# The last step of a fused Mamba-2 and expert-mixture kernel: products in another order, the last block turned by TensorE and stored as whole rows

## Chip, cores and metric

One core of one Trainium2 chip. Time is device microseconds of the whole execution, the median of several. Ratios are the mean time of one kernel's fast runs over that of the other's of the same rounds, so they are not quite the ratio of the medians quoted. The rounds of the experiments ran on two chips, each round with its own runs of the kernel before.

## The reference

Two parts after each other. The first is a state-space scan over 4 x 8 heads, whose output becomes a matrix `x` of 3072 tokens by 256. The second is four experts, which take nearly all of the time:

```python
for e in range(E):                       # E = 4, F = 1024, D = 256
    h = np.maximum(x @ w1[e], 0.0)
    out += p[:, e:e + 1] * (h @ w2[e])   # out: [3072 tokens, 256]
```

Everything is float32.

## The kernel before

Tokens go through in six blocks of 512. A block takes eight steps, and each step (but the first two of all, which use plain products) makes seven first and seven second products of half-size matrices (a Strassen-like scheme: seven products and sums in place of eight products). The second products add up in PSUM over the eight steps, and lie there transposed: 128 features on the partitions, tokens along the row. After the last step of a block the sums are combined into `o` and stored. Only the very last block has nothing behind it to hide its end; `finish` is that end.

```python
def diff(n, o, x, y):                    # VectorE, line 385: operands of products 7, 5, 6, 4
    ...
    nc.vector.tensor_sub(h[o], h[x], h[y])

ORDER = (1, 3, 7, 5, 6, 2, 4)            # where product i adds up: acc[k, index // 2], half index % 2

def smul(n, i):                          # second product i: two matmuls, four instructions (L440)
    u, half = divmod(ORDER.index(i), 2)
    ...
    rhs = hid[n][("11", "21", "22", "T4", "T1", "T2", "T3")[i - 1]]   # T3, T1, T2, T4 come from diff
    for j in range(JJ):
        nc.tensor.matmul(out=acc[k, u][:, half], lhsT=w2_op(n, w)[:, j], rhs=rhs[:, j], ...)

def finish(n):
    ...                                  # b1, b2: first and second 256 tokens
    for i in (6, 1, 3):
        smul(n, i)
    keep(k, 0)                           # ScalarE copies acc[k, 0] to SBUF
    p1, p3 = kept[k, 0][:, 0], kept[k, 0][:, 1]
    add(u[:, 0], acc[k, 2][:, 0], p1)
    add(u[:, 1], u[:, 0], p3)
    smul(n, 7)
    smul(n, 5)
    p7, p5 = acc[k, 1][:, 0], acc[k, 1][:, 1]
    add(u[:, 2], p7, u[:, 0])            # L489
    add(o[:, 1, b2], p5, u[:, 2])        # L490
    add(o[:, 0, b2], p5, u[:, 1])
    leave(k, HB, HB, (nc.sync, nc.scalar))
    smul(n, 2)
    add(o[:, 0, b1], acc[k, 2][:, 1], p1)
    smul(n, 4)
    add(o[:, 1, b1], acc[k, 3][:, 0], u[:, 2])   # L496
    leave(k, 0, HB, (nc.sync, nc.scalar))

def leave(k, lo, n, queues):
    ot = ffn.tile([P, 2, n // 32, 32], FP32, tag="ot", name="ot")
    nc.vector.transpose(ot.rearrange("p d b j -> p d (b j)"), o[:, :, lo:lo + n])   # 32x32 blocks
    dst = out[r:r + n].rearrange("(b i) (d a j) -> a d i b j", i=32, j=32, d=2)
    for q in range(P // 32):
        for d in range(2):
            queues[d].dma_start(out=dst[q, d], in_=ot[32 * q:32 * q + 32, d])       # runs of 128 B
```

`ot` holds the transposed values in blocks of 32 by 32, as its rearrangement shows, so a run of memory that can be written at once is 32 floats, 128 bytes.

Of the kernel before, what the change touches and what calls it, by code (L numbers as in the profile page):

```python
# [8 lines left out]
FP32 = mybir.dt.float32  # L9
# [3 lines left out]
P = 128  # L13
# [4 lines left out]
def kernel(  # L18
# [33 lines left out]
    nc = tc.nc  # L52

    NCH, _, W = xbc.shape
    E, DM, F = w1.shape
    NH = NQ * NT
    HN = P
    BLK = 512
    HB = BLK // 2
# [16 lines left out]
    att = ctx.enter_context(tc.tile_pool(name="att", bufs=2))  # L76
    ffn = ctx.enter_context(tc.tile_pool(name="ffn", bufs=2))
    ps_att = ctx.enter_context(tc.tile_pool(name="ps_att", bufs=2, space=bass.MemoryType.PSUM))
# [59 lines left out]
    def w2_op(n, w):  # L138

        if w < 4:  # L140
            a_, d = divmod(w, 2)
            return wt2[n][:, :4 * HB].rearrange(
                "p (a j d m) -> p a j d m", a=2, j=JJ, d=2)[:, a_, :, d]
        return wt2[n][:, w * HB:w * HB + HB].rearrange("p (j m) -> p j m", j=JJ)
# [13 lines left out]
    def sum_w2(n):  # L158
# [7 lines left out]
        out=a_sb, in_=a.rearrange("c h s -> (c h) s").rearrange("(p r) s -> p r s", r=2))  # L166
# [7 lines left out]
    ident = const.tile([P, NH, P], FP32, name="ident")  # L174
# [13 lines left out]
    for q in range(NQ):  # L188
        r = slice(32 * q, 32 * q + 32)
# [199 lines left out]
    def begin(k, u):  # L389
        if (k, u) in acc:  # L390
            return False
        acc[k, u] = ps_s.tile([P, 2, HB], FP32, tag=f"acc{u}", name=f"acc{u}")
        return True
# [19 lines left out]
    def plain_second(n, b, d):  # L413


        k = n // SPB
        u, half = {(1, 1): (2, 1), (2, 1): (3, 0), (1, 2): (0, 1), (2, 2): (3, 1)}[d, b]
        begins = begin(k, u)
        for i, w in enumerate(((A11, A12), (S3, A22))[d - 1]):
            for j in range(JJ):  # L420
                nc.tensor.matmul(  # L421
                    out=acc[k, u][:, half], lhsT=w2_op(n, w)[:, j], rhs=hid[n][f"{i + 1}{b}"][:, j],
                    start=(begins and i == 0 and j == 0), stop=False, skip_group_check=True)

    def smul(n, i):

        if n < 0:
            return
        k = n // SPB
        if n < PLAIN:  # L430
            if n == PLAIN - 1 and i in ORDER[:4]:
                m, d = divmod(ORDER.index(i), 2)
                plain_second(m, 2, d + 1)
            return
        u, half = divmod(ORDER.index(i), 2)
        begins = begin(k, u)
        w = (A11, A12, S4, A22, S1, S2, S3)[i - 1]
        rhs = hid[n][("11", "21", "22", "T4", "T1", "T2", "T3")[i - 1]]
        for j in range(JJ):
            nc.tensor.matmul(  # L440
                out=acc[k, u][:, half], lhsT=w2_op(n, w)[:, j], rhs=rhs[:, j],
                start=(begins and j == 0),
                stop=(n % SPB == SPB - 1 and j == JJ - 1), skip_group_check=True)

    kept = {}

    def keep(k, u):
        e = kept[k, u] = ffn.tile([P, 2, HB], FP32, tag=f"kept{u}", name=f"kept{u}", bufs=1)
        nc.scalar.copy(out=e, in_=acc[k, u])
# [22 lines left out]

    def finish(n):

        k = n // SPB
        add = nc.vector.tensor_add
        b1, b2 = slice(0, HB), slice(HB, BLK)
        o = kept[k, "o"] = ffn.tile([P, 2, BLK], FP32, tag="o", name="o", bufs=1)
        u = ffn.tile([P, 3, HB], FP32, tag="u", name="u", bufs=1)
        for i in (6, 1, 3):  # L480
            smul(n, i)
        keep(k, 0)
        p1, p3 = kept[k, 0][:, 0], kept[k, 0][:, 1]
        add(u[:, 0], acc[k, 2][:, 0], p1)
        add(u[:, 1], u[:, 0], p3)
        smul(n, 7)
        smul(n, 5)
        p7, p5 = acc[k, 1][:, 0], acc[k, 1][:, 1]
        add(u[:, 2], p7, u[:, 0])  # L489
        add(o[:, 1, b2], p5, u[:, 2])  # L490
        add(o[:, 0, b2], p5, u[:, 1])
        leave(k, HB, HB, (nc.sync, nc.scalar))
        smul(n, 2)
        add(o[:, 0, b1], acc[k, 2][:, 1], p1)
        smul(n, 4)
        add(o[:, 1, b1], acc[k, 3][:, 0], u[:, 2])  # L496
        leave(k, 0, HB, (nc.sync, nc.scalar))

    def leave(k, lo, n, queues):

        o = kept[k, "o"]

        ot = ffn.tile([P, 2, n // 32, 32], FP32, tag="ot", name="ot")
        nc.vector.transpose(ot.rearrange("p d b j -> p d (b j)"), o[:, :, lo:lo + n])
        r = k * BLK + lo
# [3 lines that stand above are left out]
                queues[d].dma_start(out=dst[q, d], in_=ot[32 * q:32 * q + 32, d])  # L509
# [85 lines left out]
    for n in range(PLAIN, NS):  # L595
        k, r = divmod(n, SPB)
# [67 lines left out]
        if ending:  # L664
            combine(k - 1, 2)
    finish(NS - 1)


# [43 lines left out]
```

## Time and profile before

| | before |
|---|---|
| time, median of the 3 runs before the prediction | 664.66 us (664.35 to 665.47) |
| TensorE busy | 646.3 us of 662.1, 98% |
| end of the last matmul to the end of the span | 6.7 us |
| of that, store: first issue to end | 6.4 us |

The time is TensorE's, except for a ramp at the start and this tail. The lines are in the prediction. To compare tails of different executions I use one mark in all of them, which no edit touches: the start of VectorE's last pair of differences. In the kernel before, the timeline (start, duration, engine, line, operation) has it at

```profile
648.32 1.42 DVE L385 TENSOR_TENSOR hT<-h,hT 128x512 f32<-128x512 f32 x2
```

From there to the end of the span at 662.1 is the **tail**, 13.78 us. Spans are printed to 0.1 us, so a tail may be off by 0.05; with the unrounded spans of the packed traces none below moves by more than 0.04.

### The profile page before, as it was taken

What the parts mean: (1) busy time and instruction counts of PE and PEld (TensorE: products, weight loads), DVE (VectorE), ACT (ScalarE), POOL (GpSimd) and SP (SyncE); (2) the same over time, 40 slices, a digit from 0 to 9 for tenths busy, and PEclk for the clock granted to TensorE, in tenths of its full rate; (3) what the DMA queues carried; (4) which work ended last, traced back from release to release, by engine and by line L of the source; (5) the groups of instructions that cost most, each with busy time, mean ns of one, the idle gap of its engine ahead of it and who ended that gap; (6) DMA issues with size and microseconds to landing.
All of it is one profiled execution on the core that took longest, in us unless ns stands there. A gap on an engine that the chain in (4) does not pass through costs nothing.

```text
span 662.1 us, 8709 instructions
## 1 busy us (share of the span) xinstructions
PE 646.3 (98%) x3333; PEld 537.5 (81%) x3333; DVE 491.9 (74%) x788; ACT 114.2 (17%) x244; POOL 110.7 (17%) x153
## 2 busy tenths in 40 slices
PE   7999999999999999999999999999999999999995
PEld 2687887888888888888888888888888888888884
DVE  6857898788687688776878776868868767856554
ACT  2001111221112122111121111112211211111110
POOL 2587795030000002000003000002100000200000
PEclk9999999999999999999999999999999999999999
DMA  8985998636736444755372765454673543563102
GB/s 251 342 331 218 335 345 317 218 156 192 258 128 260 158 153 128 299 193 183 148 258 68 254 224 181 184 183 167 182 264 125 194 166 112 153 244 112 55 1 32
DMA packets 70937, 128.62 MB, mean 194 GB/s; under 512 B 29040, under 2 KB 52464, under 8 KB 70896
## 3 DMA queue, kind: packets, MB, share of 16 engines
q1 hardware_dynamic: 65968, 112.79, 49.9%
q0 software_dynamic: 2304, 14.68, 5.6%
q10 hardware_dynamic: 2624, 0.61, 0.4%
q8 instruction: 26, 0.43, 0.3%
q14 instruction: 15, 0.12, 0.1%
HBM read 109.99 MB, written 18.07 MB: 193 GB/s over the span
## 4 chain that ended last, share of the span: by engine, by line
PE 86%; DVE 8%; issue 1%; DMA 1%; DVEq 0%; SPq 0%
PE acc L440 38%; PE X L356 22%; PE Y L356 18%; DVE hT L385 3%; PE acc L421 2%; PE g L273 2%; PE y L301 1%; DVE MT L283 1%; DVE LT L239 1%; PE y L295 1%; DMA wt<-w_d 1%; PE X L404 1%; PE Y L404 1%; DVE z L368 1%; DVE h L378 1%
## 5 line engine op out<-in xcount | busy, mean ns | idle before, releaser
L440 PE MATMUL acc<-hT,wt 128*128 128x256 f32 x736 | 183.4, 382 | 0.8 <-DVE hT L385 0.8
L368 DVE TENSOR_TENSOR z<-Y,snap 128x512 f32<-128x512 f32 x138 | 95.0, 688 | 112.7 <-ACT snap L363 87.3
L363 ACT COPY snap<-X 128x512 f32<-128x512 f32 x138 | 80.8, 586 | 469.1 <-PE X L356 467.1
L440 PEld LDWEIGHTS acc<-hT,wt 128*128 128x128 f32 x736 | 138.2, 190 | 25.5 <-issue 6.3
L356 PE MATMUL X<-yS,wt 128*128 128x256 f32 x552 | 141.7, 379 | 0.0
L440 PE MATMUL acc<-h,wt 128*128 128x256 f32 x552 | 141.5, 379 | 0.0
L440 PEld LDWEIGHTS acc<-h,wt 128*128 128x128 f32 x552 | 104.9, 190 | 14.3
L356 PEld LDWEIGHTS X<-yS,wt 128*128 128x128 f32 x552 | 104.9, 190 | 14.3
L378 DVE SCALAR_TENSOR_TENSOR h<-z,gate 128x512 f32<-128x512 f32 x138 | 97.3, 705 | 3.1
L356 PE MATMUL Y<-yT,wt 128*128 128x256 f32 x368 | 94.7, 380 | 0.7 <-DVE z L368 0.6
L356 PEld LDWEIGHTS Y<-yT,wt 128*128 128x128 f32 x368 | 68.6, 190 | 12.3 <-DVE z L368 1.5
L385 DVE TENSOR_TENSOR hT<-h,hT 128x512 f32<-128x512 f32 x92 | 70.7, 768 | 3.2
L385 DVE TENSOR_TENSOR hT<-h,h 128x512 f32<-128x512 f32 x92 | 62.7, 718 | 0.7
L246 POOL TENSOR_TENSOR MT<-xb,LT 128x128 f32<-128x128 f32 x20 | 8.3, 414 | 318.0 <-issue 142.4
L239 DVE TENSOR_TENSOR_SCAN LT<-ab,ident 128x1024 f32<-128x1024 f32 x24 | 55.9, 2329 | 0.4
L356 PE MATMUL Y<-yS,wt 128*128 128x256 f32 x184 | 49.4, 391 | 2.1 <-DVE z L368 2.0
L283 DVE TENSOR_TENSOR MT<-g,LT 128x256 f32<-128x256 f32 x96 | 34.0, 416 | 21.0 <-PE g L273 20.8
L356 PE MATMUL X<-yT,wt 128*128 128x256 f32 x184 | 47.3, 380 | 0.5 <-DVE MT L283 0.5
L356 PEld LDWEIGHTS Y<-yS,wt 128*128 128x128 f32 x184 | 33.2, 189 | 11.0 <-DVE z L368 4.2
L378 DVE SCALAR_TENSOR_TENSOR h<-X,gate 128x512 f32<-128x512 f32 x50 | 34.5, 691 | 9.6 <-PE X L356 5.7
L356 PEld LDWEIGHTS X<-yT,wt 128*128 128x128 f32 x184 | 34.9, 190 | 5.6 <-DVE MT L283 0.9
L257 POOL TENSOR_TENSOR cts<-ctm,dec 128x256 f32<-128x256 f32 x20 | 14.6, 732 | 70.9 <-DVE dec L254 70.5
(77 smaller groups left out, 330.4 us busy)
## 6 DMA issues: line engine op xcount, KB each, us to landing
wt<-w_d SPq DMA_DIRECT2D x80, 896.0 KB, 6.2
w_d<-wt POOLq DMA_DIRECT2D x16, 896.0 KB, 6.2
ab<-acut_d SPq DMA_DIRECT2D x22, 512.0 KB, 9.8
wt<-in_w_dram SPq DMA_DIRECT2D x32, 256.0 KB, 5.6
xb<-in_xbc_dram SPq DMA_DIRECT2D x24, 320.0 KB
gate<-p_d SPq DMA_DIRECT2D x24, 256.0 KB, 6.0
out_dram<-ot SPq DMA_DIRECT2D x40, 64.0 KB, 2.0
ah<-ac_d SPq DMA_DIRECT2D x19, 64.0 KB
```

The lines of the kernel that those rows point to most:

```text
L239: nc.vector.tensor_tensor_scan(out=LT, data0=s["ab"], data1=ident.rearrange("p h s -> p (h s)"), initial=0.0, op0=ALU.mult, op1=ALU.add)
L257: nc.gpsimd.tensor_mul(cts, s["ctm"], dec.unsqueeze(1).to_broadcast([HN, NT, P]))
L273: nc.tensor.matmul(out=g.rearrange("p t s -> p (t s)"), lhsT=s["xb"][k, OBT:OBT + P], rhs=s["ctm"][k].rearrange("p t s -> p (t s)"), start ...
L283: nc.vector.tensor_mul(s["MT"][:, h, 0:P], s["g"][q], s["LT"][:, h])
L356: nc.tensor.matmul(out=f[bank][:, j], lhsT=wt1[n][:, w, j * P:j * P + P], rhs=rhs, start=(i in (1, 2, 5) and j == 0), stop=(j == JJ - 1), ...
L363: nc.scalar.copy(out=s, in_=first[n]["X"])
L368: nc.vector.tensor_add(z, first[n]["Y"], first[n][i])
L378: nc.vector.scalar_tensor_tensor(out=h, in0=first[n][src], scalar=0.0, in1=g.unsqueeze(1).to_broadcast([P, JJ, HB]), op0=ALU.max, op1=ALU. ...
L385: nc.vector.tensor_sub(h[o], h[x], h[y])
L404: nc.tensor.matmul(out=f[bank][:, j], lhsT=wt1[n][:, w, j * P:j * P + P], rhs=yT[k][:, i, cols], start=(i == 0 and j == 0), stop=(i == 1), ...
L421: nc.tensor.matmul(out=acc[k, u][:, half], lhsT=w2_op(n, w)[:, j], rhs=hid[n][f"{i + 1}{b}"][:, j], start=(begins and i == 0 and j == 0), ...
L440: nc.tensor.matmul(out=acc[k, u][:, half], lhsT=w2_op(n, w)[:, j], rhs=rhs[:, j], start=(begins and j == 0), stop=(n % SPB == SPB - 1 and ...
```

## The change

The intent: start the last seven products without the wait for a difference; drop the stream transposes and the sixteen stores of short runs; let TensorE turn `o` in full 128 by 128 blocks, so that a token's 256 features stand as one row of 1 KB, and store in three transfers.

```diff
-        for i in (6, 1, 3):
-            smul(n, i)
+        smul(n, 1)
+        smul(n, 3)
         keep(k, 0)
         p1, p3 = kept[k, 0][:, 0], kept[k, 0][:, 1]
+        smul(n, 6)
 ...
+        def turn_out(b, d):
+            if b not in turned:
+                turned[b] = ps_att.tile([P, 2, DM], FP32, tag="att", name="turned")
+                rows[b] = ffn.tile([P, 2, DM], FP32, tag="rows", name="rows")
+            for i in range(2):
+                lo = b * HB + i * P
+                nc.tensor.transpose(
+                    turned[b][:, i, d * P:d * P + P], o[:, d, lo:lo + P], ident[:, 0])
 ...
-        leave(k, HB, HB, (nc.sync, nc.scalar))
         smul(n, 2)
         add(o[:, 0, b1], acc[k, 2][:, 1], p1)
+        turn_out(1, 1)
         smul(n, 4)
+        turn_out(1, 0)
+        nc.scalar.copy(out=rows[1], in_=turned[1])
+        nc.sync.dma_start(out=dst(1), in_=rows[1])
+        turn_out(0, 0)
         add(o[:, 1, b1], acc[k, 3][:, 0], u[:, 2])
-        leave(k, 0, HB, (nc.sync, nc.scalar))
+        turn_out(0, 1)
+        nc.vector.tensor_copy(rows[0][:, 0], turned[0][:, 0])
+        nc.sync.dma_start(out=dst(0)[:, 0], in_=rows[0][:, 0])
+        nc.scalar.copy(out=rows[0][:, 1], in_=turned[0][:, 1])
+        nc.scalar.dma_start(out=dst(0)[:, 1], in_=rows[0][:, 1])
```

`dst(b)` is the 256 rows of that half, as `(i p) m -> p i m`. "First half" below is b = 0, "second half" is b = 1; the second is ready first.

More of the change, by code (lines that the diff above doesn't have):

```diff
@@ L477, in finish, with dst @@
         b1, b2 = slice(0, HB), slice(HB, BLK)
-        o = kept[k, "o"] = ffn.tile([P, 2, BLK], FP32, tag="o", name="o", bufs=1)
+        o = ffn.tile([P, 2, BLK], FP32, tag="o", name="o", bufs=1)
         u = ffn.tile([P, 3, HB], FP32, tag="u", name="u", bufs=1)
-        for i in (6, 1, 3):
-            smul(n, i)
+        turned, rows = {}, {}
+        def turn_out(b, d):
[6 more added lines that the diff above has]
+                    turned[b][:, i, d * P:d * P + P], o[:, d, lo:lo + P], ident[:, 0])
+        def dst(b):
+            r = k * BLK + b * HB
+            return out[r:r + HB].rearrange("(i p) m -> p i m", p=P)
+        smul(n, 1)
+        smul(n, 3)
         keep(k, 0)
         p1, p3 = kept[k, 0][:, 0], kept[k, 0][:, 1]
+        smul(n, 6)
         add(u[:, 0], acc[k, 2][:, 0], p1)
```

## The prediction

> **What bounds the kernel now.** I read the engine shares first, then the last 22 us of the timeline, because the change touches only the last of the steps. The page says that TensorE is the bound of the whole:
>
> ```profile
> PE 646.3 (98%) x3333; PEld 537.5 (81%) x3333; DVE 491.9 (74%) x788; ACT 114.2 (17%) x244; POOL 110.7 (17%) x153
> PE 86%; DVE 8%; issue 1%; DMA 1%; DVEq 0%; SPq 0%
> ```
>
> The first line is busy time of 662.1 us, the second the chain that ended last. Nothing in the change shortens the 98%; it can only shorten the tail after the matmuls. The comparison of instruction order shows the same: up to the last step each engine has the same instructions, in the same order, with the same waits. The timeline of the end, columns start, duration, engine, line, operation:
>
> ```profile
> 649.06 1.13 PE L440 MATMUL acc<-hT,wt 128*128 128x256 f32 x4 [0.85 <-DVE hT L385]
> ...
> 652.01 0.59 ACT L449 COPY kept<-acc 128x512 f32<-128x512 f32 x1 [9.22 <-PE acc L440]
> 652.63 0.42 DVE L484 TENSOR_TENSOR u<-acc,kept 128x256 f32<-128x256 f32 x1 [2.90 <-ACT kept L449]
> ...
> 653.68 0.42 DVE L489 TENSOR_TENSOR u<-acc,u 128x256 f32<-128x256 f32 x1 [0.17 <-PE acc L440]
> 654.14 0.42 DVE L490 TENSOR_TENSOR o<-acc,u 128x256 f32<-128x256 f32 x1
> 654.35 1.03 PE L440 MATMUL acc<-hT,wt 128*128 128x256 f32 x4
> ...
> 655.67 3.85 SPq L509 DMA_DIRECT2D out_dram<-ot  x8
> 655.67 3.94 ACTq L509 DMA_DIRECT2D out_dram<-ot  x8
> 655.88 0.41 DVE L496 TENSOR_TENSOR o<-acc,u 128x256 f32<-128x256 f32 x1
> 656.32 0.71 DVE L504 STREAM_TRANSPOSE ot<-o 128x512 f32<-128x512 f32 x1
> ```
>
> TensorE starts the last seven products at 649.06 after a wait of 0.85, because product 6, put first, needs a difference that VectorE ends at 649.02. It ends at 655.38. VectorE is done at 657.03. The last 5 us are the store: eight issues on each of two queues, until 659.6. The stretches and the DMA view from 640 on show what the transfers do:
>
> ```profile
> 657.10:659.70 2.60, 0.00 (x0) 0.00 (x0) 0.00 (x0) 0.00 (x0) 0.00 (x0) 1.00 0.85 132
> 659.70:662.10 2.40, 0.00 (x0) 0.00 (x0) 0.00 (x0) 0.00 (x0) 0.00 (x0) 0.72 0.30 47
> DMA packets 4352, 0.53 MB, mean 23 GB/s; under 512 B 4352, under 2 KB 4352, under 8 KB 4352
> ```
>
> The last two columns of the stretches are the DMA share and GB/s: engines 85% busy at only 132 GB/s, with every packet small (0.53 MB over 4352 is about 122 B). Data begins at 656.5, 0.83 after the first issue, and ends at about 660.7; at 131 GB/s 0.53 MB needs 4.0 us, which is that. So the end is bound by 128-byte stores, not by issuing. The wait of the sync queue agrees:
>
> ```profile
> SPq L708 <- DMA out_dram<-ot: 1.2, 1, 1.2
> ```
>
> It waited 1.2 us after its last issue, to 660.8; semaphores and a barrier of all engines fill the 1.3 us to 662.1, and stay.
>
> **What the Trainium skill says.** "DMA: Bandwidth & Descriptors", Specifications, names 512 B as the smallest transfer that reaches line rate. The trace agrees in kind: 131 GB/s here, with 128 B, while from 8.5 to 10.5 us packets mostly of 512 B and more ran at 334 GB/s. "TensorE: Matmul & The Clock Gate", Part 4, says that a TensorE transpose does 128x128 at once, lands in PSUM and needs a copy after, about 275 ns in a kernel for bf16. The one transpose in this trace, 96 columns of f32, has 314 ns and a weight load of 124, so 128 columns would load in about 165 (an estimate, 124 x 128/96). "PSUM — Partial Sum Buffer", PSUM bank collisions, says that two engines may not touch one bank in the same partitions at once, and that the compiler orders them. In the changed program ScalarE's copy of the second half waits for VectorE's copy of the first, as that would ask: both halves lie in one bank. No run yet shows its cost.
>
> **The change, part by part.**
>
> Order of products. 1 and 3 need only what is ready, so TensorE starts at 648.21 instead of 649.06, and 6 comes third at 649.94, past 649.02. A product takes 0.86 (four instructions of 0.215), its result is there 1.03 after it starts, and consumers began 0.13 (VectorE) to 0.19 (ScalarE) later. So product 5 starts at 651.66, product 2 at 652.53 and ends at 653.39. Gain 0.85 for all that follows.
>
> VectorE before the first transpose. The add of L489 waited for product 5, not 7 (653.55 + 0.13 = 653.68). In the new order: 651.66 + 1.03 + 0.13 = 652.82, then the o add of the second half ends 0.88 later (654.56 − 653.68) at 653.70, the next at 654.04, and the first half's first at about 654.45. No stream transpose lies between them any more: 0.71 twice is gone, and with it what delayed L496 by about 0.5.
>
> Transposes on TensorE. Eight of them, in four pairs. The first pair stands ahead of product 4 and waits until 653.75, so TensorE stands 0.35; then two weight loads of about 0.18 and that of product 4 before its first multiply, at 654.29. That gives back 0.05 of a 0.85 gain: product 4 began at 654.24 before. Its result: 654.29 + 1.03 = 655.32. The pairs for (second half, 0) and (first half, 0) run behind it, to about 655.85, beside the last add, which takes 655.45 to 655.86. The last pair starts at 655.90: two loads, then a multiply of 0.31, and 0.1 until seen, 0.36 + 0.31 + 0.1, so 656.65.
>
> Copies. ScalarE's copy of the second half (128x512; 0.586 for the same shape at L363) starts at about 655.8, ends at 656.4. VectorE's of 128x256 out of PSUM: 0.40, as its adds, to 657.05. ScalarE's then, 0.37 as at L308: to 657.45.
>
> Stores. 512 KB in three transfers instead of sixteen, 1 KB runs. Issues at 656.42 and 657.07 (sync), 657.5 (scalar); data 0.83 later: 657.25, 657.90 and 658.33. At some 300 GB/s (the mean of 4 to 12 us in this trace was 307) 256 KB take 0.87 and 128 KB 0.44, so the three end at 658.12, 658.56 and 659.0. The last transfer is no longer bound by the bandwidth but by its own late issue. Landing seen 0.1 after, 659.1, plus the unchanged 1.3: 660.4 to 660.5 in place of 662.1.
>
> Sum, by what ends the tail: the last block was turned at 657.03, and is now at 656.65, −0.4 (the order's gain is spent on the first pair's stall, so this comes from the two stream transposes). The two copies in a row that TensorE's transpose needs, +0.8. From the last write to SBUF to the landing 1.65 instead of 3.8, −2.1. Total about −1.7 us, 0.26% of the time. Predicted 664.66 − 1.7 = 663.0.
>
> **Rivals.**
>
> First, the tail becomes a chain of small steps. Add, transposes, two copies and an issue each hand over by semaphore; each handover that costs 0.1 to 0.2 more, or transposes that take 0.3 each instead of 0.18 at the margin, would eat 0.5 to 1.0. For it: nearly half of my sum is handovers, and the first pair stalls TensorE just where the old kernel ran. Against it: 0.02 to 0.17 is what the chain shows. It would make 663.5 to 664.0, no visible change.
>
> Second, the transfers are not faster. Stores of 1 KB into memory by themselves are nowhere in this trace; the 307 GB/s are mostly loads with much in flight. If the landing is a fixed latency near the 1.9 to 2.0 us seen from issue to landing for 32 and 64 KB pieces, the last lands at 657.5 + 2.0 = 659.5: 663.4. This is the one I fear most. At 131 GB/s still, 512 KB from 657.25 would end at 661.2, slower by 0.5: 665.1. The small packets with busy engines speak against that.
>
> Third, it goes better: data of 256 KB runs at 400 GB/s (slices of 422 and 436 stand around 158 us), transposes pack at half a matmul's time, the semaphores at the end shrink with sixteen transfers fewer. Then the landing is at 658.4, and the time 662.2.
>
> **Range and chances.** The middle is 663.0. The rivals put it between 662.2 and 664.0; the three runs before spread over 1.1 us by themselves, which I add in part: 661.8 to 664.4. A gain of over 2% would be 13 us, all of the span from the first of the seven products to the end. A loss of 2% would need a new wait of 13 us in an unchanged program, or a slow run. Faster 0.005, same 0.99, slower 0.005.
>
> **What would show it.** In the profile after: the products of the last step start with no wait on VectorE; product 4's matmuls start within 0.3 us of where they did; no packets of under 512 B after 650 us; the stretch with DMA is under 2 us long instead of 4.2; ScalarE's second copy starts just as VectorE's ends; from the last landing to the end is again 1.3. It is wrong if TensorE stands over 0.5 us at the first pair, if a pair takes over 0.7, if the last issue to landing is over 2 us, or if the time is above 664.4 with nothing changed before 648 us.

## The result, and the profile after

The median went from 664.5 us (4 runs) to 662.0 (4 runs, 661.11 to 663.06); ratio 0.9962, 95% interval 0.9939 to 0.9986. That is 2.5 us less, within 2%, and it is not a chance difference. Six more runs of the same kernel, on another occasion, gave 0.9977 (0.9962 to 0.9992). The tail went from 13.78 to 11.40 us, so 2.4 less. The other 0.4 between the two profiled spans (662.1 and 659.3) lies ahead of the mark, in unchanged instructions, and is not the change's. The first store is issued as late as before, 7.36 after the mark against 7.35: what the new order of products saves, the transposes and copies take up, and all of the 2.4 is won behind that issue.

The timeline after, from the mark on:

```profile
647.63 1.89 PE L440 MATMUL acc<-h,wt 128*128 128x256 f32 x8
647.90 1.42 DVE L385 TENSOR_TENSOR hT<-h,hT 128x512 f32<-128x512 f32 x2
649.36 2.75 PE L440 MATMUL acc<-hT,wt 128*128 128x256 f32 x12
...
652.15 0.42 DVE L506 TENSOR_TENSOR u<-acc,u 128x256 f32<-128x256 f32 x1 [0.77 <-PE acc L440]
652.61 0.42 DVE L507 TENSOR_TENSOR o<-acc,u 128x256 f32<-128x256 f32 x1
...
653.09 0.20 PEld L489 LDWEIGHTS turned<-ident,o 128*128 128x128 f32 x2 [0.51 <-DVE o L507]
653.09 0.44 PE L489 MATMUL turned<-ident,o 128*128 128x128 f32 x2
...
653.36 1.03 PE L440 MATMUL acc<-hT,wt 128*128 128x256 f32 x4
...
654.43 0.42 DVE L517 TENSOR_TENSOR o<-acc,u 128x256 f32<-128x256 f32 x1 [0.73 <-PE acc L440]
654.65 0.59 ACT L514 COPY rows<-turned 128x512 f32<-128x512 f32 x1 [4.45 <-PE turned L489]
654.91 0.20 PEld L489 LDWEIGHTS turned<-ident,o 128*128 128x128 f32 x2 [0.32 <-DVE o L517]
655.26 0.39 SPq L515 DMA_DIRECT2D out_dram<-rows  x1
655.38 0.42 DVE L519 COPY rows<-turned 128x256 f32<-128x256 f32 x1 [0.53 <-PE turned L489]
655.84 0.34 SPq L520 DMA_DIRECT2D out_dram<-rows  x1
655.84 0.37 ACT L521 COPY rows<-turned 128x256 f32<-128x256 f32 x1 [0.61 <-DVE rows L519]
656.24 0.37 ACTq L522 DMA_DIRECT2D out_dram<-rows  x1
```

Read it in this order. TensorE's first products (x8, without a wait in brackets) start 0.27 ahead of the mark; before, the first started 0.74 after it. The weight load at 653.09 waited 0.51 for VectorE: that is the first pair of transposes, for which TensorE stands. (The 0.51 counts from the end of the last weight load. Product 2 began at 651.95, so the next multiply could have begun 0.86 later, at 652.81: TensorE lost 0.28.) Product 4 starts 0.27 after the pair. Then add, last pair, VectorE's copy and ScalarE's follow with gaps of 0.03 to 0.06. ScalarE's copy of the same bank starts at 655.84, when VectorE's is done (655.80), and ends at 656.21. "PSUM — Partial Sum Buffer" of the Trainium skill, PSUM bank collisions, says that two engines may not access one bank in the same partitions at the same time, and here they do not. Both copies also write one SBUF tile, `rows`, and no run parts the two reasons.

The DMA view from 640 on, and the sync queue's waits:

```profile
DMA packets 560, 0.52 MB, mean 26 GB/s; under 512 B 48, under 2 KB 560, under 8 KB 560
...
SPq L733 <- DMA out_dram<-rows: 1.8, 3, 1.1
```

560 packets in place of 4352: 512 rows, and 48 of under 512 B, which are 16 for each of the three transfers (256 for sixteen transfers, in a run below). The GB/s row of that view stands at 346 and 342 in full slices, where it was about 131. In short windows of that view data starts at 656.16, 0.9 after the first issue, and is over at 657.78. In between, the data flowed without a pause. The last transfer lands 1.9 us after its issue at 656.24, about 658.14, and 1.16 of semaphores and barrier follow.

### The profile page after: what moved, and what is told of

It is laid out like the page before. It is cut to its first block, busy times and chain, and to the rows that moved or that the text cites. A ratio compares the mean times of both kernels' runs of the same rounds, so it can differ in the third digit from the quotient of the medians.

```text
span 659.3 us, 8708 instructions
## 1 busy us (share of the span) xinstructions
PE 647.0 (98%) x3341; PEld 538.3 (82%) x3341; DVE 490.4 (74%) x787; ACT 115.3 (17%) x246; POOL 111.6 (17%) x153
## 4 chain that ended last, share of the span: by engine, by line
PE 87%; DVE 7%; issue 1%; DMA 1%; ACT 0%; DVEq 0%; SPq 0%
PE acc L440 39%; PE X L356 22%; PE Y L356 18%; DVE hT L385 2%; PE acc L421 2%; PE g L273 2%; PE y L301 1%; DVE MT L283 1%; DVE LT L239 1%; PE y L295 1%; DMA wt<-w_d 1%; PE X L404 1%; PE Y L404 1%; DVE z L368 1%; DVE h L378 1%
```

## The experiments

"Tail" is as above; "first issue" and "last issue" are counted from the mark as well. The small differences in tail may be read, as the control at the end shows; the times have intervals of about 0.2%, 1.3 us, and only say the same more coarsely.

### Order of products alone

```diff
 # the kernel before
-        for i in (6, 1, 3):
+        for i in (1, 3):
             smul(n, i)
         keep(k, 0)
+        smul(n, 6)
```

> The kernel before with the new order of products only (1, 3, 6, ...), its stream transposes and sixteen stores unchanged. The tail is counted from the start of the last pair of VectorE's differences (L385) to the end of the span: 13.8 us before (648.32 to 662.1), 11.4 after (647.90 to 659.3). Theory A, the store is set by when its first piece can be issued: product 5 ends 0.86 earlier, so the first issue does, and the tail is 12.9; time about 0.13% less. Theory B, my prediction's sum, in which the order's gain is used up: tail 13.8.

Tail 12.77, time 0.9972 of before (0.9951 to 0.9993). Mark and issues in its timeline, span 663.4:

```profile
650.63 1.42 DVE L385 TENSOR_TENSOR hT<-h,hT 128x512 f32<-128x512 f32 x2
...
656.87 3.86 SPq L510 DMA_DIRECT2D out_dram<-ot  x8
```

The first issue is 6.24 after the mark; it was 7.35. Theory A holds, and the order alone is worth 1.0 us in the tail and 1.11 at the first issue. It is more than the 0.85 that the profile called idle. That number runs from the modelled end of the matmul before, which stands after the moment when TensorE could take the next one: a product's end is shown as start + 1.03, and the next product starts at + 0.86. That is 0.17 more, and 0.11 was lost after the wait as well, as the first product took 0.97 to the next one (649.06 to 650.03). Together 1.13: against the mark the first of the seven products started 1.00 earlier, and product 4 1.11 earlier (4.92 in place of 6.03).

### Transposes and stores alone

```diff
 # the changed kernel
-        smul(n, 1)
-        smul(n, 3)
+        for i in (6, 1, 3):
+            smul(n, i)
         keep(k, 0)
         p1, p3 = kept[k, 0][:, 0], kept[k, 0][:, 1]
-        smul(n, 6)
```

> The changed kernel with the old order of products (6, 1, 3, ...). Theory A: everything after the products is 0.85 later, tail 12.3 in place of 11.4; time 0.25% below before. Theory B, the stall of TensorE at the first pair of transposes takes the gain of the order in any case: tail 11.4 to 11.5.

Tail 12.55, time 0.9967 (0.9949 to 0.9985): 1.15 longer than the changed kernel, 1.23 shorter than before. From its timeline (span 661.9):

```profile
649.35 1.42 DVE L385 TENSOR_TENSOR hT<-h,hT 128x512 f32<-128x512 f32 x2
...
657.82 0.39 SPq L514 DMA_DIRECT2D out_dram<-rows  x1
```

Its first issue is 8.47 after the mark, 1.11 later than the changed kernel's. Theory B falls: the order's gain goes all the way through to the end. The two parts nearly add: 1.01 and 1.23 against 2.38.

### The first pair of transposes behind product 4

```diff
-        turn_out(1, 1)
         smul(n, 4)
+        turn_out(1, 1)
         turn_out(1, 0)
```

> The changed kernel with the first pair of transposes moved behind product 4, so that TensorE does not stand 0.51 us before it. Theory A, the stall passes on to the end: product 4 starts 0.38 earlier (652.98 instead of 653.36), three pairs fit beside VectorE's last add, tail 11.0. Theory B, six transposes in a row last longer than the 0.9 us between product 4's end and the last add's end, and the last pair waits for them: tail 11.3 to 11.6.

Tail 11.14, time 0.9956 (0.9936 to 0.9977). Theory A, though with 0.26 of the 0.4, and although product 4 started 0.54 earlier against the mark (4.92 in place of 5.46) and not 0.38. From its timeline (span 659.0):

```profile
652.78 1.03 PE L440 MATMUL acc<-hT,wt 128*128 128x256 f32 x4
...
653.64 1.12 PE L489 MATMUL turned<-ident,o 128*128 128x128 f32 x8
653.84 0.42 DVE L517 TENSOR_TENSOR o<-acc,u 128x256 f32<-128x256 f32 x1 [0.18 <-PE acc L440]
```

All eight transposes, the last pair's wait for the add included, fit in 1.12 us. The first six start 0.11 apart, the sixth at 654.19, before the add ends at 654.26.

### Two banks for the last copies

```diff
+        own = [ps_f.tile([P, DM], FP32, tag=t, name="own") for t in ("X", "Y")]
+        row = [ffn.tile([P, DM], FP32, tag=f"row{i}", name="row", bufs=1) for i in range(2)]
 ...                                       # turn_out(0, d) writes own[0] and own[1]
-        nc.vector.tensor_copy(rows[0][:, 0], turned[0][:, 0])
-        nc.sync.dma_start(out=dst(0)[:, 0], in_=rows[0][:, 0])
-        nc.scalar.copy(out=rows[0][:, 1], in_=turned[0][:, 1])
-        nc.scalar.dma_start(out=dst(0)[:, 1], in_=rows[0][:, 1])
+        nc.vector.tensor_copy(row[0], own[0])
+        nc.sync.dma_start(out=dst(0)[:, 0], in_=row[0])
+        nc.scalar.copy(out=row[1], in_=own[1])
+        nc.scalar.dma_start(out=dst(0)[:, 1], in_=row[1])
```

> The changed kernel with the two halves of the first block turned into two PSUM banks (X and Y, free by then) and copied to two SBUF tiles, so that VectorE's and ScalarE's copies run at the same time. Theory A, the copies in a row are on the path: the last issue starts 0.4 earlier, tail 11.0. Theory B, the landing is set by the transfers' own rate: the last bytes come at the same time, tail 11.3 to 11.4.

Tail 11.51, no shorter; time 0.9965 (0.9945 to 0.9984). The copies did run together, and the last issue came earlier (mark 650.09, span 661.6):

```profile
657.47 0.42 DVE L522 COPY row<-own 128x256 f32<-128x256 f32 x1 [0.42 <-PE own L490]
657.57 0.37 ACT L524 COPY row<-own 128x256 f32<-128x256 f32 x1 [0.15 <-PE own L490]
657.93 0.42 SPq L523 DMA_DIRECT2D out_dram<-row  x1
657.98 0.37 ACTq L525 DMA_DIRECT2D out_dram<-row  x1
```

The last issue is 7.89 after the mark in place of 8.34. The view gives 2.2 us from issue to landing for the sync queue's transfer; the scalar queue's, issued last, landed 2.4 after its issue by the semaphore events in the trace, in place of 1.9. What was won in the copies was lost in the transfer: theory B. The data began and ended where they did in the changed kernel, 8.26 and 9.9 after the mark. The first issue, 7.36, had not moved at all.

### Both edits

The two diffs above together.

> The changed kernel with both edits, the first pair of transposes behind product 4 and two PSUM banks. If the two steps follow one another on the path the gains add: tail 10.6 (11.4 - 0.4 - 0.4), time about 0.5% below before. If one hides the other: tail 11.0.

Tail 11.07, time 0.9955 (0.9935 to 0.9974). Only what the late pair gives; the banks hide. Against the mark the first issue is at 7.02, the last at 7.50, and the landing comes 2.4 after it. Over all kernels with rows of 1 KB and all of the data in three transfers, the end came 4.0 to 4.2 us after the *first* issue (4.04, 4.08, 4.11, 4.15, 4.05), wherever the last one stood; the control at the end has 4.06.

### Short pieces, few transfers

```diff
-                rows[b] = ffn.tile([P, 2, DM], FP32, tag="rows", name="rows")
+                rows[b] = ffn.tile([P, 2, 8, 33], FP32, tag="rows", name="rows")[:, :, :, 0:32]
 ...                    # copies and transfers by (p, g, m) with m = 32; the second half in two transfers
```

> The changed kernel with rows padded in SBUF to 33 floats in 32, so that the stores go in pieces of 128 B; four transfers in place of three (the second half's is cut in two), the same bytes and nearly the same issue times. Theory A, the old store was bound by its small packets at 131 GB/s: 512 KB take 4.0 us from the first data, tail 13.5 to 13.9. Theory B, it was bound by sixteen issues of 0.49 us in two queues: tail 11.4 to 11.7.

Tail 13.89, time 1.0005 (0.9984 to 1.0025): with 128 B pieces the stores give back all that the change won. Its DMA view:

```profile
DMA packets 4160, 0.52 MB, mean 28 GB/s; under 512 B 4160, under 2 KB 4160, under 8 KB 4160
q1 hardware_dynamic: 3120, 0.39, 12.9%
q10 hardware_dynamic: 1040, 0.13, 4.1%
```

The data ran at 135 to 149 GB/s in full slices. A transfer also cost the issuing queue 0.65 in place of 0.39. Theory A. The rows lie whole in memory here and only the pieces in SBUF are short, yet the rate is nearly that of the kernel before: it goes with the size of the pieces, not with where they lie.

### Whole rows, many transfers

```diff
-        nc.sync.dma_start(out=dst(1), in_=rows[1])
+        def many(q, i, b, queue):
+            s = slice(32 * q, 32 * q + 32)
+            queue.dma_start(out=dst(b)[s, i], in_=rows[b][s, i])
+        for q in range(4):
+            many(q, 0, 1, nc.sync)
+            many(q, 1, 1, nc.scalar)
 ...                    # the first half likewise; both of its copies on VectorE
```

> The changed kernel with sixteen transfers of 32 KB, eight on each queue as before, in rows of 1 KB (both copies of the first half on VectorE, as ScalarE issues). Theory A, packets: the data is moved as it comes, tail 11.4 to 11.8. Theory B, issues: the eighth issue of a queue starts 7 x 0.47 = 3.3 us after the first at 655.26, lands 1.9 later, tail 13.8.

Tail 13.50, time 1.0003 (0.9979 to 1.0027). The issues alone also give back nearly all:

```profile
656.77 3.64 SPq L517 DMA_DIRECT2D out_dram<-rows  x8
656.77 3.70 ACTq L517 DMA_DIRECT2D out_dram<-rows  x8
```

and the data behind them ran at 136 to 145 GB/s with the engines about half busy. Theory B. So the two runs together say neither "packets" nor "issues": in the kernel before both were at about the same height, 4.0 us of data and 3.9 of issuing, and by these two runs taking away one alone wins 0.3 at most. The comparison is fair, as the first issue comes 7.35 after the mark in the kernel before, 7.36 and 7.37 in these two. The change had to take both.

### A small last transfer

```diff
-        nc.scalar.dma_start(out=dst(0)[:, 1], in_=rows[0][:, 1])
+        nc.scalar.dma_start(out=dst(0)[0:16, 1], in_=rows[0][0:16, 1])
```

> The changed kernel whose last transfer stores 16 of 128 rows, 16 KB in place of 128 (wrong on purpose: 112 rows of the result are not written). Theory A, the last landing is a fixed latency of 1.9 us from the issue: tail 11.3 to 11.4, and 1.8 to 1.9 from issue to landing. Theory B, it is the transfer's time: the last 0.3 to 0.4 us of data go, tail 11.0.

Wrong, as 112 rows are not written. Tail 11.30, issue to landing 1.8, time 0.9979 (0.9958 to 1.0001). Seven eighths of the last transfer gone wins 0.1 (0.18 with unrounded spans). Even 16 KB take 1.8 us from issue to landing (32 KB took 1.7 in the run before), so in the changed kernel this time and the data in front end at nearly the same moment.

### The late pair, two banks, and the second half in two pieces

```diff
 # both edits, and
-        nc.scalar.copy(out=rows[1], in_=turned[1])
-        nc.sync.dma_start(out=dst(1), in_=rows[1])
+        for i in range(2):
+            nc.scalar.copy(out=rows[1][:, i], in_=turned[1][:, i])
+            nc.sync.dma_start(out=dst(1)[:, i], in_=rows[1][:, i])
```

> The kernel with both edits (late pair, two banks) whose second half is also copied and stored in two pieces of 128 KB, so that the first issue comes some 0.2 earlier. Revised theory: the tail ends at the later of two, the last issue + 1.8 + 1.15, and the first issue + 0.85 + the bytes at 345 GB/s (1.5) + 0.55 + 1.15 = 4.05. In the two-edit kernel the first issue came 7.02 after the anchor and the tail was 11.07; here 6.8, tail 10.85. Rival, the last issue alone sets the end: it moves by nothing, tail 11.1.

Tail 10.91, as the revised theory had it (10.85). From its timeline (span 659.0):

```profile
648.09 1.42 DVE L385 TENSOR_TENSOR hT<-h,hT 128x512 f32<-128x512 f32 x2
...
654.90 0.81 SPq L519 DMA_DIRECT2D out_dram<-rows  x2
...
655.81 0.40 SPq L524 DMA_DIRECT2D out_dram<-row  x1
```

The first issue is at 6.81 after the mark. The last is at 7.72, which is 0.22 *later* than in the kernel with both edits, and the end still came earlier. The time is 661.0 (5 runs, 660.63 to 661.14), ratio 0.9949 (0.9935 to 0.9963) to before: the lowest of all kernels here, though the intervals of several overlap. It is correct, and in tail 0.5 better than the changed kernel. Its median is 2.0 lower than that of the control of the same rounds, 663.0; the tails account for 0.5 of that, and the rest lies in instructions that are the same.

### A small first transfer

```diff
 # both edits, and
-        nc.sync.dma_start(out=dst(1), in_=rows[1])
+        nc.sync.dma_start(out=dst(1)[0:16], in_=rows[1][0:16])
```

> The two-edit kernel whose first transfer stores 16 of 128 partitions, 32 KB in place of 256 (wrong on purpose). Revised theory, the data ahead in the queues held the end back: without it the last issue's latency is what is left, 7.5 + 1.8 + 1.15 = 10.45. Rival, the gain of the earlier last issue was lost in something else, such as two queues landing together: tail stays at 11.0 to 11.1.

Its output is wrong, which doesn't matter for the time. Tail 10.66 against 11.07, issue to landing 2.1 against 2.4; time 0.9965 (0.9946 to 0.9984). The mechanism is shown: data put in *ahead* of the last transfers held them back by 0.4. The size is not quite: 10.45 was expected. The DMA view tells where the other 0.2 probably lies. The queues' packets from 658.5 to 658.8, and from 658.8 to 659.1:

```profile
q10 hardware_dynamic: 92, 0.09, 91.0%
q1 hardware_dynamic: 2, 0.00, 0.4%
...
q1 hardware_dynamic: 68, 0.07, 68.8%
q10 hardware_dynamic: 49, 0.03, 36.0%
```

q10 is the scalar queue, q1 the sync queue. The sync queue's transfer, issued last, had its data behind the scalar queue's 128 KB. No run takes those away too, so the 0.2 is argued and not shown.

### The changed kernel again

> The changed kernel once more, unaltered, as a control of how well the tail repeats: 11.4 within 0.1, time 0.3 to 0.4% below before. If the tail differs by over 0.2, the small differences between the other runs are not to be read.

Tail 11.42 (mark 650.18, span 661.6) against 11.40. The tail repeats within 0.02, while the mark itself came 2.3 us later than in the first profile of the same kernel. Time 0.9977 (0.9962 to 0.9992), where 0.3 to 0.4% below was expected.

## Why the prediction was right, and where its steps were not

The predicted time was 663.0, in 661.8 to 664.4; measured 662.0. The class and the range held, and so did the mechanism in the main: the gain lies in the store. The size did not quite: 1.7 predicted, 2.4 in the tail. The time alone could not tell these apart: its intervals are 0.9 to 4.1 us in the first round and 0.5 to 2.5 in the control's, whose median, 663.0, is the predicted one. That 663.0 came within 1.0 is partly luck, as below. Its steps:

- **What bounds the kernel, and no change before the last step:** held. TensorE is 98% busy after as before.
- **"The end is bound by 128-byte stores, not by issuing":** half wrong. Few transfers of short pieces bring the old tail back (13.89), and so do many transfers of whole rows (13.50). Both limits were there. The prediction set the 4.0 us of data beside the span and stopped at the agreement; the eight issues of 3.85 us on the line above agreed as well.
- **Order of products, 0.85:** too small. 1.01 by adding it, 1.15 by taking it away. The idle time counts from a modelled matmul end, which misses 0.17, and the first product after the wait lost 0.11 more. The prediction counted product starts at 0.86 each from 649.06, past that 0.11, and so had product 4 at 654.24 where its own line has 654.35, and 0.13 from a result to VectorE where it was 0.03.
- **"That gives back 0.05 of a 0.85 gain: product 4 began at 654.24 before" and, in the sum, "the order's gain is spent on the first pair's stall":** this is the step that failed. Against the mark product 4 was to start at 5.97; it started at 5.46, and at 6.03 before, so it gained 0.57. Of the 0.51 between forecast and measurement, 0.25 is the order's larger gain (the add of L506 started at 4.25 in place of 4.50). The rest is the weight loads: the prediction took 0.18 for each, in a row, and so 0.54 from the pair's start to product 4's. It took 0.27. The stall is real, but costs only 0.26 at the end, as the kernel without it shows.
- **The last pair, 0.75 from its start to the copy:** measured 0.47 (654.91 to 655.38). Together with the point before, "the last block was turned at 657.03, and is now at 656.65, −0.4" is the mis-sized term: from the mark it went from 8.71 to 7.48, so −1.23. That is 0.83 more than the −0.4 predicted (0.51 at product 4, 0.28 at the last pair, the rest in small parts); the store's term gives back 0.12 and the copies' 0.03, which leaves the 0.68 between 1.7 and 2.38.
- **Two copies in a row, +0.8:** 0.83 by the timeline. But they were not on the path in the way the sum has it: with the copies side by side the tail was no shorter.
- **The store from the last write to SBUF, −2.1:** from 657.03 to 662.1 is 5.07, from 656.21 to 659.3 is 3.09: −1.98. That the sum came so close is luck in part, as its terms erred in opposite ways. Landing was to be seen 0.1 after the data and took 0.36; the data ran at about 340 in place of 300 GB/s, and the end after the landing took 1.16 in place of 1.3.
- **"The last transfer is no longer bound by the bandwidth but by its own late issue":** no, or at most equally. A last transfer of an eighth wins 0.1 to 0.2, an earlier last issue nothing. The end is the later of two: the last issue plus a landing of 1.8, and the first issue plus 0.9 until data flows, 1.6 us of data and 0.36 more (the expectations split these a little otherwise, with nearly the same sum). This rule was made after the first eight experiments; it foretold one run well (10.85, measured 10.91) and one 0.2 too low (10.45, measured 10.66). In the changed kernel the two differ by little, which is why moving the last issue alone does nothing.
- **Rivals:** the second, a fixed landing of 1.9 to 2.0, fits the changed kernel (1.9), and would have given 663.4 only because all before it was put too late; but the landing is not fixed, as 2.4 with two banks shows. The first, dear handovers, fell: they were 0.03 to 0.06. The third had a time of 662.2, nearest to what came, for a reason it gave in part: the transposes do pack at half a matmul's time (0.11 between starts, against 0.215), but the data ran at 340 GB/s and not at 400.
- **Its signs:** no wait on VectorE at the first products, under 2 us of data (1.6), ScalarE's second copy just behind VectorE's, and about 1.3 at the end (1.16) came true. Product 4 within 0.3 us of where it was did not (0.57 earlier), nor did "no packets of under 512 B" (48 small ones came with the transfers). The sign of being wrong, TensorE standing over 0.5 us at the first pair, is met only by the weight load's wait (0.51); TensorE lost 0.28.

## What to carry to other kernels

When a tail of stores shows busy DMA engines and also a full row of issues, ask of each what the end would be if only the other were gone; where both give the same number, shortening one wins nothing. In a tail, the *first* store's issue matters as much as the last one's, since everything behind it waits for its data: issue the part that is ready first as early as it can go; here, cutting it in two pieces won 0.2. To measure a microsecond in 660, count from a mark which the edit cannot move.

## What the Trainium skill lacked or had wrong

- "DMA: Bandwidth & Descriptors", Issuing engines are not separate DMA queues, says of the time to initiate a DMA that it "is usually small relative to the DMA itself". This is a case outside its "usually": 32 KB stores in rows of 1 KB took about 0.43 us of a queue each, 3.7 us for eight, while their data at 340 GB/s would be 0.1 us each (an estimate from the changed kernel's rate), and the tail grew from 11.4 to 13.5 us.
- The same page, Specifications, gives 512 B as the smallest transfer for line rate, but no rate for stores of 128 B on this chip. Stores of 128 B ran at about 130 to 149 GB/s, of 1 KB at about 340 to 350, from one core.
- The same page measures its fixed cost of about 2 us on the GpSimd path, and shows no such measurement for the sync and scalar queues. For stores from these, issue to landing was 1.7 to 1.9 us for 16 to 128 KB, and up to 2.4 in the kernels that issued the last transfer earlier behind the same data. The first-byte latency in its Specifications, about 0.6 us for these queues, was 0.83 before and 0.9 after from the first issue's start, and so longer.
- "TensorE: Matmul & The Clock Gate", Part 4, has a duration for bf16 transposes and no pace. Here 128x128 in f32 showed 272 ns each by the profile, two of them 0.44 together, six in a row 0.11 from start to start, and the next product's first matmul started 0.27 after the first of a pair. The part says that the full clock does not engage for transposes; the granted clock was 1.00 from 652 to 657 us, among matmuls, so no run here shows that.
